# Moving work of the first blocks off VectorE: maxima and masks to TensorE, low parts of weights and numerators to accumulating transfers

## The chip, the cores and the metric

The kernel runs on one core of a Trainium2 chip. The metric is device time in microseconds (us) of one launch, as the median of several runs. The engines have one instruction queue each and run it strictly in order: TensorE (PE in the profile; PEld is its weight load), VectorE (DVE), ScalarE (ACT), GpSimd (POOL) and SyncE (SP). In this kernel SP and POOL only issue transfers (DMAs), apart from a few fills by POOL at the start. Transfers that add into their destination ("accumulating") are issued by POOL.

## The reference, cut to what matters

```python
B, H, S, D = 8, 8, 576, 64
# attention: two parts, added
s  = scale * q_d @ k_d.T                      # q, k, v averaged over groups of 4 rows: 144 x 144
out_d = softmax(s) @ v_d                      # repeated 4 times along the rows
s  = where(|row - col| < 4, scale * q @ k.T, -1e9)
out_local = softmax(s) @ v                    # softmax subtracts the row's maximum, divides by sum + 1e-9
x = (repeat(out_d, 4) + out_local).transpose(0, 2, 1, 3).reshape(4608, 512)
# two-layer network with a rational activation
h = x @ w_in                                  # 512 x 2048
P = a0 + a1*h + a2*h**2 + a3*h**3
Q = 1 + |b0|*|h| + |b1|*h**2
out = (P / (Q + 1e-6)) @ w_out                # 2048 x 512
```

The weights come as 64-bit floats; everything else is 32-bit. All products are carried with close to 32-bit accuracy.

## The kernel before, in words

**Blocks and steps.** The 4608 rows of x are cut into nine blocks of 512: the first 512 rows of each of the eight batches, and a ninth with the 64 rows that each batch leaves over. A block has 16 steps, one for each 128 columns of `w_in`; step n makes `h(n)` (128 x 512, in one of two PSUM banks), `middle(n)` makes the activation from it, and `o(n)` multiplies it with 128 rows of `w_out` and adds into four PSUM banks. `o(n)` stands two steps behind `h(n)` (`LAG`). There are 144 steps.

**Accuracy by two parts.** Fast matmuls take operands rounded to a shorter type (float32r). So each operand is split into a high part (the rounded value) and a low part (what the rounding left), and three products are added: high x high, low x high, high x low, 12 matmuls of 128 x 512 for `h(n)` (L843) and 12 for `o(n)` (L923). Block 0 (steps below `NAT` = 16) makes `h` otherwise: with the unsplit 32-bit `w_in` and x, in 4 slow matmuls (L831, two records each).

**Weights.** `weights(w, f, spot)` fetches 1 MB of 64-bit weights (two steps' worth) into a staging place, and ScalarE (L356) and VectorE (L359, L362) put the exact 32-bit value together from the two halves (`wb`). `parts` splits it: ScalarE copies it into the high tile `wh` (L376), VectorE subtracts, low = exact - high (L379). For `w_out` this is done at once, for `w_in` after block 0 has used the exact value. The exact value lies in the room of the low part.

**Middle.** `middle(n)` has four ScalarE reads of the PSUM bank (|h|, h squared, a3*h+a2, a1*h+a0, all L856), a logarithm and an exponential for the reciprocal of Q, and seven VectorE operations: L871, then the numerator in L876 (multiply by h squared) and L877 (add `u` = a1*h+a0), then L883 (the high part of the activation, `g`), L886, L891, L892 (its low part).

**Attention.** The local scores are made in ten windows of 64 rows per pair of heads, 128 x 640 in two PSUM banks. In batch 0 (the start, before any `h`) `scores` adds the mask on TensorE: four matmuls with an identity (L440) write it into the banks first. `softmax_local` then takes the negative maxima on VectorE (L482), scales them, and ScalarE runs ten small exponentials per pair, 128 x 64 each, with the maximum as bias and the sum taken along (L497). In the other batches `Half.scores` lets VectorE add the mask while it copies the scores out of PSUM (L637), takes maxima (L648), and the ten exponentials read SBUF (L659). `normalize` multiplies by the reciprocal sums: the local part on VectorE, the pooled part on ScalarE (L540), or on VectorE (L548) for the batches in `EP_DVE`, which is batch 0. The mean over 4 rows for the pooled part comes from four loads, three of them accumulating (L419); batch 0 reduces on VectorE (L428). `attend(b)` for batch b+2 is spread over the steps of block b+1, batch 1 over block 0.

**What sets the order.** Every operation is given to a planner with an engine, an assumed cost, what it reads and writes, and here and there a due time. `Plan.run` simulates the engines, taking on each the ready task that is latest against its due time, and this writes one fixed order into each engine's queue. So a change of a cost, a due time (`H0`, `H_FIRST`, `QUAD_GAP`) or a dependence reorders everything; what happens at run time is then decided by the queues and the semaphores alone.

Of the kernel before, what the change touches and what calls it, by code (L numbers as in the profile page):

```python
# [9 lines left out]
F32 = mybir.dt.float32  # L10
BF16 = mybir.dt.bfloat16
# [9 lines left out]
P = 128  # L21
# [162 lines left out]
def attention_moe(  # L184
# [45 lines left out]
    high2, low2, bits2 = [[], []], [[], []], [[], []]  # L230
    for name, parts in (("wh", high2), ("wl", low2)):
        for w in range(2):
            for f in range(0, NFC, 2):
                t = put(f"{name}{w}_{f}", [P, 2, NCC, P], F32R)
                parts[w].append(t)
                if parts is low2:
                    bits2[w].append(put(f"wb{w}_{f}", [P, 2, NCC, P], I32, t.at))
    high, low, bits = (
        [[part(x[w][f // 2], x[w][f // 2].ap[:, f % 2], f % 2 * 4 * DM, 4 * DM) for f in range(NFC)] for w in range(2)]
        for x in (high2, low2, bits2)  # L240
    )

# [10 lines left out]
    maskb = put("maskb", [P, 2, NW // 2 * D], BF16, mt[0].at)  # L253
# [43 lines left out]
    arena = nc.alloc_sbuf_tensor("arena", [P, (top - base) // 4 + 16], I32)  # L297
# [45 lines left out]
    def weights(w, f, spot, due=None):  # L343
        st = spot.ap.rearrange("p n (c f two) -> p n c f two", two=2, c=NCC)
        lo, word = low2[w][f // 2], bits2[w][f // 2]
# [23 lines left out]
        add("DVE", 0.6, upper, (spot,), (lo,))  # L369
        add("DVE", 1.13, lower, (spot, lo), (lo,))  # L370
        if f >= (WO if w else NAT):
            parts(w, f)

    def parts(w, f, due=None):
        hi, lo, word = high2[w][f // 2], low2[w][f // 2], bits2[w][f // 2]
        add("ACT", 0.88, lambda: nc.scalar.copy(out=hi.ap, in_=word.ap.bitcast(F32)), (lo,), (hi,), due=due)  # L376
        add(
            "DVE", 1.13,
            lambda: nc.vector.tensor_tensor(  # L379
                out=lo.ap, in0=word.ap.bitcast(F32), in1=hi.ap.bitcast(F32), op=ALU.subtract  # L380
            ),
            (lo, hi), (lo,), due=due,
        )
# [92 lines left out]
    def softmax_local(c, bk):  # L476
        s = c.slot
        nm, sm = s.nm.ap, s.sm.ap
        view = two(bk)[:, :, : NW // 2 * D].rearrange("p j (c k) -> p j c k", k=D)
# [6 lines left out]
        )  # L486
        add(
# [331 lines left out]
    def h_part(n, f):  # L819
# [5 lines left out]
        if n < NAT:  # L825

            x = xsf[blk.slot][1]
            for c in range(NCC):

                def issue(c=c):  # L830
                    nc.tensor.matmul(  # L831
                        ph.ap, lhsT=bits[0][fc].ap[:, c, :].bitcast(F32), rhs=x.ap[:, c, :],
# [3 lines left out]
                add("PE", 0.858, issue, (low[0][fc], part(x, None, 4 * c * t, 4 * t)), (ph,), due=due_h(n) + 0.05 * c)  # L836
# [21 lines left out]
    def middle(n):  # L858
# [18 lines left out]
        add("DVE", 0.61, lambda: v.tensor_tensor(out=ta.ap, in0=ta.ap, in1=u.ap, op=ALU.add), (ta, u), (ta,))  # L877
        act(0.63, log, tb, tb.ap, AF.Ln, bias=cone)
        act(0.54, tq, log, log.ap, AF.Exp, scale=-1.0)
        if n < WO:  # L880
# [291 lines left out]
```

## Time and profile before

| | |
|---|---|
| median of 3 runs | 971.1 us (970.48 to 972.1) |
| the profiled execution's own time | 970.52 us |
| its span in the trace | 968.5 us |
| TensorE busy | 943.4 us (97%) |
| VectorE busy | 857.2 us (89%) |
| ScalarE busy | 818.0 us (84%) |
| GpSimd busy | 113.8 us (12%) |
| granted TensorE clock, mean | 0.995 |

How to read it: busy times are unions of instruction times; ends of matmuls are modelled, so a TensorE that is paced by waits can still read as busy. "Idle before" is the time in which an engine stood still ahead of an instruction, with the instruction that released it. Lines (L923) are lines of the kernel's file; a group in the profile is one line, engine and shape.

### The profile page before, as it was taken

The page shows a single profiled execution, that of the slowest core. Times are in us where ns is not written, and L with a number is a line of the kernel's source. Part 1 is how long each engine was busy: PE and PEld are TensorE (multiplying, and loading weights), DVE is VectorE, ACT ScalarE, POOL GpSimd, SP SyncE. Part 2 cuts the span into 40 slices and gives each one's busy share as a digit, 9 for nine tenths or more (in the row PEclk, how much of TensorE's full clock was granted, in tenths as well). Part 3 has the DMA queues.
Part 4 walks back from the last instruction along what each step waited for, and adds up shares of the span by engine and source line. Part 5 has one row for each costly group of instructions (what it writes and reads, how often), then busy time and mean ns, then how long its engine had stood idle before and what let it go on. Part 6 is the DMA issues. An engine that isn't in the chain of part 4 may idle for free.

```text
span 968.5 us, 19358 instructions
## 1 busy us (share of the span) xinstructions
PE 943.4 (97%) x7182; PEld 739.6 (76%) x7182; DVE 857.2 (89%) x1450; ACT 818.0 (84%) x2056; POOL 113.8 (12%) x136
## 2 busy tenths in 40 slices
PE   7899999999999999999999999999999999999996
PEld 5555657787877788788877887778878888888885
DVE  6899999999888989898889888898979899988885
ACT  6899898988889897979798978988797977778774
POOL 1212121111202020212111110202021000000000
PEclk9999999999999999999999999999999999999998
DMA  9985453333433344434333433334332010001001
GB/s 296 350 279 118 137 147 85 98 70 83 74 102 57 100 65 110 75 82 75 89 89 72 94 70 106 55 103 72 94 72 57 2 44 1 1 1 44 0 1 44
DMA packets 43166, 85.06 MB, mean 88 GB/s; under 512 B 4864, under 2 KB 25728, under 8 KB 43072
## 3 DMA queue, kind: packets, MB, share of 16 engines
q1 hardware_dynamic: 25344, 63.52, 19.8%
q0 software_dynamic: 17728, 20.31, 15.3%
q8 instruction: 57, 0.93, 0.4%
q14 instruction: 37, 0.30, 0.1%
HBM read 74.37 MB, written 9.44 MB: 87 GB/s over the span
## 4 chain that ended last, share of the span: by engine, by line
PE 40%; DVE 27%; ACT 25%; issue 6%; DMA 1%; DVEq 0%; POOL 0%; ACTq 0%; POOLq 0%; SPq 0%
PE psum L923 18%; PE psum L843 17%; ACT m L856 7%; ACT el L659 7%; DVE g L883 4%; DVE m L886 3%; DVE m L891 3%; ACT epc L523 3%; DVE g L892 3%; DVE m L876 3%; DVE m L871 3%; DVE m L877 3%; ACT gb L856 2%; ACT epc L540 2%; PE psum L831 2%
## 5 line engine op out<-in xcount | busy, mean ns | idle before, releaser
L923 PE MATMUL psum<-wh,g 128*128 128x512 f32 x1152 | 392.9, 404 | 3.2 <-DVE g L892 1.5
L856 ACT ACTIVATE m<-psum,cf 128x512 f32<-128x512 f32 x288 | 212.0, 740 | 63.5 <-PE psum L843 59.4
L923 PEld LDWEIGHTS psum<-wh,g 128*128 128x128 f32 x1152 | 214.1, 188 | 60.6 <-DVE g L892 6.6
L843 PE MATMUL psum<-xs,wh 128*128 128x512 f32 x1024 | 258.8, 393 | 0.1
L923 PE MATMUL psum<-wl,g 128*128 128x512 f32 x576 | 224.3, 390 | 0.0
L843 PEld LDWEIGHTS psum<-xs,wh 128*128 128x128 f32 x1024 | 189.8, 188 | 42.7 <-issue 2.2
L883 DVE TENSOR_TENSOR g<-m,m 128x512 fp32r<-128x512 f32 x144 | 99.5, 691 | 69.0 <-ACT m L856 62.4
L843 PE MATMUL psum<-xs,wl 128*128 128x512 f32 x512 | 137.7, 391 | 0.0
L856 ACT ACTIVATE gb<-psum,cf 128x512 f32<-128x512 f32 x144 | 114.5, 795 | 15.8 <-PE psum L923 15.8
L923 PEld LDWEIGHTS psum<-wl,g 128*128 128x128 f32 x576 | 108.2, 188 | 23.0 <-issue 1.4
L856 ACT ACTIVATE gb<-m,cf 128x512 f32<-128x512 f32 x144 | 106.3, 738 | 19.4 <-DVE m L871 16.8
L419 POOL DMA_DIRECT2D pq<-in_qkp_dram x84 | 74.5, 932 | 389.1 <-DMA pq<-in_qkp_dram 352.0
L856 ACT ACTIVATE m<-gb 128x512 f32<-128x512 f32 x144 | 92.6, 643 | 24.9 <-DVE m L876 23.3
L843 PEld LDWEIGHTS psum<-xs,wl 128*128 128x128 f32 x512 | 95.7, 188 | 20.1
L871 DVE SCALAR_TENSOR_TENSOR m<-m,cf,m 128x512 f32<-128x512 f32 x144 | 107.3, 745 | 1.7 <-ACT m L856 1.6
L877 DVE TENSOR_TENSOR m<-m,gb 128x512 f32<-128x512 f32 x144 | 99.1, 688 | 6.6 <-ACT gb L856 0.4
L886 DVE SCALAR_TENSOR_TENSOR m<-m,g 128x512 f32<-128x512 f32 x144 | 99.4, 690 | 3.5
L892 DVE TENSOR_TENSOR g<-m,m 128x512 fp32r<-128x512 f32 x144 | 98.8, 686 | 2.8
L891 DVE TENSOR_TENSOR m<-m,m 128x512 f32<-128x512 f32 x144 | 99.0, 688 | 2.2
L876 DVE TENSOR_TENSOR m<-m,m 128x512 f32<-128x512 f32 x144 | 98.6, 685 | 0.0
L659 ACT ACTIVATE el<-el,nm 128x64 f32<-128x64 f32 x280 | 93.5, 338 | 3.8 <-DVE nm L653 2.7
L856 ACT ACTIVATE m<-psum 128x512 f32<-128x512 f32 x144 | 86.9, 603 | 0.0
(71 smaller groups left out, 905.9 us busy)
## 6 DMA issues: line engine op xcount, KB each, us to landing
qk<-in_qk_dram SPq DMA_DIRECT2D x32, 590.0 KB, 3.9
pq<-in_qkp_dram POOLq DMA_DIRECT2D x84, 144.0 KB, 3.3
vw<-in_vw_dram SPq DMA_DIRECT2D x32, 320.0 KB, 4.0
out_dram<-xf SPq DMA_DIRECT2D x32, 256.0 KB, 2.4
vpc<-in_vp_dram POOLq DMA_DIRECT2D x42, 168.0 KB, 3.6
sx<-in_w_in_dram SPq DMA_DIRECT2D x5, 1024.0 KB, 13.7
sl<-in_w_out_dram SPq DMA_DIRECT2D x4, 1024.0 KB, 9.5
sx<-in_w_out_dram SPq DMA_DIRECT2D x4, 1024.0 KB, 5.3
```

Of the source, the lines that this page charges most:

```text
L419: lambda d=dst, x=x: nc.gpsimd.dma_start(out=d.ap, in_=x, accum_op=ALU.add),
L659: nc.scalar.activation(out=e[:, n], in_=e[:, n], func=AF.Exp, bias=nm[:, n : n + 1], scale=scale, accum_out=sm[:, n : n + 1],)
L843: nc.tensor.matmul(ph.ap[:, f * t : (f + 1) * t], lhsT=(high, low)[j][0][fc].ap[:, c, :], rhs=blk.x[i].ap[:, c, :] if blk.b is not None el ...
L856: add("ACT", cost, lambda: nc.scalar.activation(out=out_.ap, in_=in_, func=func, **kw), (room_in, cf, *more), (out_,))
L871: lambda: v.scalar_tensor_tensor(out=tb.ap, in0=tq.ap, scalar=b1, in1=tb.ap, op0=ALU.mult, op1=ALU.add),
L876: add("DVE", 0.61, lambda: v.tensor_tensor(out=ta.ap, in0=ta.ap, in1=tq.ap, op=ALU.mult), (ta, tq), (ta,))
L877: add("DVE", 0.61, lambda: v.tensor_tensor(out=ta.ap, in0=ta.ap, in1=u.ap, op=ALU.add), (ta, u), (ta,))
L883: add("DVE", 0.61, lambda: v.tensor_tensor(out=gh.ap, in0=ta.ap, in1=tq.ap, op=ALU.mult), (ta, tq), (gh,))
L886: lambda: v.scalar_tensor_tensor(out=tb.ap, in0=tb.ap, scalar=CONE, in1=gh.ap.bitcast(F32), op0=ALU.add, op1=ALU.mult),
L891: add("DVE", 0.61, lambda: v.tensor_tensor(out=tb.ap, in0=ta.ap, in1=tb.ap, op=ALU.subtract), (ta, tb), (tb,))
L892: add("DVE", 0.61, lambda: v.tensor_tensor(out=gl.ap, in0=tb.ap, in1=tq.ap, op=ALU.mult), (tb, tq), (gl,))
L923: nc.tensor.matmul(ob[sub].ap, lhsT=g[i].ap[:, f0 : f0 + P], rhs=flat((high, low)[j][1][fc].ap), start=(fc == 0 and m == 0), stop=(fc == N ...
```

## The change

Five things are moved, and the planner's numbers are new:

1. Batch 0's softmax (`MINUS`, pairs 0 to 3): two 32-bit matmuls per pair add the negative maxima to the scores in PSUM (`minus`, L542 in the new file). ScalarE then runs two exponentials of 128 x 320 per pair (L549) instead of ten of 128 x 64; VectorE loses the scaling of the maxima and gains a sum over 128 x 640 (L557).
2. Batches 1 and 2 (`PEMASK`) take `scores` and `softmax_local` as batch 0 did: mask by four TensorE matmuls (L491), maxima and ten exponentials from PSUM, no masked copy by VectorE. The two banks stay taken until the exponentials have read them.
3. Low parts of `w_in` (8 pairs of steps): the exact value now lies in the high part's room. ScalarE writes -high into the low room (L424), a transfer adds the exact value (L411), and ScalarE rounds the high room in place later. VectorE's subtraction is gone. For `w_out`, f = 4 to 12 (5 pairs), the exact value lies in the next pair's low room, ScalarE makes high, VectorE writes -high (L390, one input instead of two), and a transfer adds.
4. Numerators of steps 6 to 23 (`UN`): the addition of `u` is a transfer (L954) instead of a VectorE operation.
5. Batch 1's pooled part is normalized on VectorE (`EP_DVE`).

```diff
 def weights(w, f, spot, due=None):
+    whole = f < (0 if w else NAT)
+    added = not whole and ADDED[w] <= f < NFC - 2
+    room = low2[w][f // 2 + 1] if added else (high2 if whole else low2)[w][f // 2]
+    word = aside[w][f // 2 + 1] if added else bits2[w][f // 2]
...
+    if added:
+        add("ACT", 0.88, lambda: nc.scalar.copy(out=hi.ap, in_=word.ap.bitcast(F32)), (room,), (hi,))
+        add("DVE", 0.6, lambda: nc.vector.tensor_single_scalar(out=lo.ap, in_=hi.ap.bitcast(F32), scalar=-1.0, op=ALU.mult), (hi,), (lo,))
+        accumulate(lo, word, room)
...
+def accumulate(lo, word, room, due=None):
+    add("POOL", 1.0, lambda: nc.gpsimd.dma_start(out=flat2(lo), in_=flat2(word).bitcast(F32), accum_op=ALU.add),
+        (room, lo), (lo,), due=due, lag=ALAG)
 def parts(w, f, due=None):                     # DEFER == 1
-    add("ACT", 0.88, lambda: nc.scalar.copy(out=hi.ap, in_=word.ap.bitcast(F32)), (lo,), (hi,), due=due)
-    add("DVE", 1.13, ... lo = word - hi ...)
+    add("ACT", 0.88, lambda: nc.scalar.mul(out=lo.ap, in_=exact, mul=-1.0), (hi,), (lo,), due=due)
+    accumulate(lo, word, hi, due)
+    add("ACT", 0.88, lambda: nc.scalar.copy(out=hi.ap, in_=exact), (hi,), (hi,), due=due)
...
 def softmax_local(c, bk):                      # after the maxima, for pairs in MINUS
+    def minus(j):
+        nc.tensor.matmul(view[:, j], lhsT=ident.ap, rhs=nm[:, 5 * j : 5 * j + 5].unsqueeze(2).broadcast_to([P, NW // 2, D]),
+                         start=False, stop=True, skip_group_check=True)
+    def whole(j):
+        nc.scalar.activation(out=s.el.ap[:, :, c.pos(j), :], in_=view[:, j], func=AF.Exp, scale=scale)
+    for j in range(2): add("PE", 0.56, lambda j=j: minus(j), (s.nm, ident), (bk[j],))
+    for j in range(2): add("ACT", 0.4, lambda j=j: whole(j), (bk[j],), (s.el,))
+    add("DVE", 0.74, ... sm = sum of el ...)
...
 def middle(n):
-    add("DVE", 0.61, lambda: v.tensor_tensor(out=ta.ap, in0=ta.ap, in1=u.ap, op=ALU.add), (ta, u), (ta,))
+    if UN[0] <= n < UN[1]:
+        add("POOL", 0.95, lambda: nc.gpsimd.dma_start(out=ta.ap, in_=u.ap, accum_op=ALU.add), (ta, u), (ta,), lag=ULAG)
+    else: ... as before
...
 def attend(b):
-                half_.scores(c, bk)
+                if b in PEMASK:
+                    scores(c, bk)
+                    softmax_local(c, bk)
+                else:
+                    half_.scores(c, bk)
...
-H0 = 25.89
-H_FIRST = 6.93
+H0 = 16.61
+H_FIRST = 7.57
-QUAD_GAP = 43.57
+QUAD_GAP = 43.21
-EP_DVE = (0,)
+EP_DVE = (0, 1)
+ULAG = 5.0
+UN = (6, 24)
+ALAG = 6.5
+DEFER = 1
+MINUS = (0, 1, 2, 3)
+ADDED = (99, 4)
+PEMASK = (1, 2)
```

How the order moves, at three places. In these rows a name ends in its buffer's number, `out<-in`; numbers differ between the two kernels. First ScalarE's queue from the first exponentials on (`el` is the local, `epc` the pooled exponentials of the pairs of batch 0, `eptc` and `et` their transposes). Before:

```order
L497 ACTIVATE el_151,sm_140<-psum,nm_136 128x64 x5
L497 ACTIVATE el_156,sm_141<-psum,nm_137 128x64 x5
L497 ACTIVATE el_151,sm_140<-psum,nm_136 128x64 x5
L497 ACTIVATE el_156,sm_141<-psum,nm_137 128x64 x5
L497 ACTIVATE el_162,sm_142<-psum,nm_138 128x64 x5
L523 ACTIVATE epc_146,sm_140<-psum,nm_136 128x3x48 x3
L523 ACTIVATE epc_146,sm_141<-psum,nm_137 128x3x48 x3
L497 ACTIVATE el_162,sm_142<-psum,nm_138 128x64 x5
```

and now:

```order
L549 ACTIVATE el_167<-psum 128x5x64 x2
L549 ACTIVATE el_172<-psum 128x5x64 x2
L599 ACTIVATE epc_162,sm_156<-psum,nm_152 128x3x48 x3
L599 ACTIVATE epc_162,sm_157<-psum,nm_153 128x3x48 x3
L549 ACTIVATE el_178<-psum 128x5x64
L549 ACTIVATE el_183<-psum 128x5x64
L549 ACTIVATE el_178<-psum 128x5x64
L549 ACTIVATE el_183<-psum 128x5x64
L363 ACTIVATE sx_189<-sx_189 128x1024
```

Forty small exponentials have become eight, and the first weights' conversion (L363) now follows them directly.

Second VectorE's queue between the two halves of batch 0: the normalization of the second half (`sm`, `epc`, `el`), the first weights (`wb`), the outputs of the first half (`xf`). Before, from the last normalization on:

```order
L548 TENSOR_TENSOR epc_169<-epc_169,sm_143 128x9x48
L558 TENSOR_TENSOR el_167<-el_167,sm_143 128x640
L359 TENSOR_SCALAR wb_0_73<-sx_173 128x1024
L359 TENSOR_SCALAR wb_0_89<-sl_175 128x1024
L362 SCALAR_TENSOR_TENSOR wb_0_73<-sx_173,wb_0_73 128x1024
L590 TENSOR_TENSOR xf_1_107<-psum,up_144 128x48
```

and now:

```order
L624 TENSOR_TENSOR epc_185<-epc_185,sm_159 128x9x48
L634 TENSOR_TENSOR el_183<-el_183,sm_159 128x640
L340 MEMSET cf 128x1
L366 TENSOR_SCALAR wb_0_65<-sl_191 128x1024
L366 TENSOR_SCALAR wb_2_83<-sx_190 128x1024
L666 TENSOR_TENSOR xf_1_123<-psum,up_160 128x48
```

The first weight pair (`wb_0_81` in the new file) is converted ahead of this normalization and no longer between it and the outputs.

Third GpSimd's queue where the numerators begin. Rows with `pq` and `vpc` are the accumulating loads of batch 1's second half. Before:

```order
L419 DMA vpc<-in_vp_dram 112x384
L419 DMA pq_149<-in_qkp_dram 128x288
L419 DMA pq_154<-in_qkp_dram 128x288
L419 DMA pq_149<-in_qkp_dram 128x288
L419 DMA pq_154<-in_qkp_dram 128x288
```

and now, with the low part of `w_out` (`wl_6_70`) and the numerators of steps 6, 7 and 8 (`m_132`, `m_133`, `m_132`):

```order
L411 DMA wl_6_70<-wa_4_116 128x1024
L954 DMA m_132<-gb_142 128x512
L470 DMA pq_165<-in_qkp_dram 128x288
L470 DMA pq_170<-in_qkp_dram 128x288
L470 DMA pq_165<-in_qkp_dram 128x288
L470 DMA pq_170<-in_qkp_dram 128x288
L954 DMA m_133<-gb_143 128x512
L470 DMA pq_165<-in_qkp_dram 128x288
L954 DMA m_132<-gb_142 128x512
```

Between two steps' numerators stand loads that wait for the ones ahead of them.

More of the change, by code (lines that the diff above doesn't have):

```diff
@@ L252, in attention_moe @@
     identb = put("identb", [P, P], BF16)
[L253 removed]
+    maskb = put("maskb", [P, 2, NW // 2 * D], BF16)
     maskd = put("maskd", [P, NW // 2, D], BF16)
@@ L368, in weights @@
         add("ACT", 0.94, scaled, (spot,), (spot,))
[L369 to L372, printed above, removed]
+        add("DVE", 0.6, upper, (spot,), (room,))
+        add("DVE", 1.13, lower, (spot, room), (room,))
+        if added:
+            hi, lo = high2[w][f // 2], low2[w][f // 2]
+            if f >= CAST:
+                add(
+                    "POOL", 1.0, lambda: nc.gpsimd.dma_start(out=flat2(hi), in_=flat2(word).bitcast(F32)),
+                    (room,), (hi,), lag=CLAG,
+                )
+            else:
+                add("ACT", 0.88, lambda: nc.scalar.copy(out=hi.ap, in_=word.ap.bitcast(F32)), (room,), (hi,))
+            if NEG:
+                add(
+                    "DVE", 0.6,
+                    lambda: nc.vector.tensor_single_scalar(
+                        out=lo.ap, in_=hi.ap.bitcast(F32), scalar=-1.0, op=ALU.mult
+                    ), (hi,), (lo,),
+                )
+            else:
+                add("ACT", 0.88, lambda: nc.scalar.mul(out=lo.ap, in_=hi.ap.bitcast(F32), mul=-1.0), (hi,), (lo,))
+            accumulate(lo, word, room)
+        elif not whole:
+            hi, lo = high2[w][f // 2], low2[w][f // 2]
+            add("ACT", 0.88, lambda: nc.scalar.copy(out=hi.ap, in_=word.ap.bitcast(F32)), (lo,), (hi,))
+            add(
+                "DVE", 1.13,
+                lambda: nc.vector.tensor_tensor(
+                    out=lo.ap, in0=word.ap.bitcast(F32), in1=hi.ap.bitcast(F32), op=ALU.subtract
+                ),
+                (lo, hi), (lo,),
+            )
@@ L486, in softmax_local @@
         )
+        if first:
+            def minus(j):
+                nc.tensor.matmul(
+                    view[:, j], lhsT=ident.ap,
+                    rhs=nm[:, 5 * j : 5 * j + 5].unsqueeze(2).broadcast_to([P, NW // 2, D]),
+                    start=False, stop=True, skip_group_check=True,
+                )
+            def whole(j):
+                nc.scalar.activation(out=s.el.ap[:, :, c.pos(j), :], in_=view[:, j], func=AF.Exp, scale=scale)
+            for j in range(2):
+                add("PE", 0.56, lambda j=j: minus(j), (s.nm, ident), (bk[j],))
+            for j in range(2):
+                add("ACT", 0.4, lambda j=j: whole(j), (bk[j],), (s.el,))
+            add(
+                "DVE", 0.74,
+                lambda: nc.vector.tensor_reduce(
+                    out=sm[:, :NW], in_=s.el.ap.rearrange("p c j k -> p (c j) k"), axis=AX, op=ALU.add
+                ),
+                (s.el,), (s.sm,),
+            )
+            return
         add(
```

70 lines of the change are left out of this document (38 added, 32 removed).

## The prediction

> **What bounds the kernel now.** I read the busy time by stretch first, then TensorE's waits, then its timeline at the start, and from there the queue of the engine it waited for. Busy time in five stretches (columns: length; busy time and count of PE, PEld, DVE, ACT, POOL; granted clock; DMA share; GB/s):
>
> ```profile
> 40.00:50.00 10.00, 7.53 (x110) 4.16 (x103) 7.56 (x12) 6.25 (x11) 3.97 (x4) 0.83 1.08 352
> 60.00:100.00 40.00, 38.41 (x236) 24.57 (x233) 39.87 (x68) 39.87 (x109) 5.28 (x6) 1.00 0.51 147
> 100.00:140.00 40.00, 38.78 (x289) 23.59 (x287) 38.72 (x67) 36.08 (x99) 8.09 (x9) 1.00 0.54 139
> 140.00:180.00 40.00, 39.22 (x320) 28.30 (x321) 38.64 (x62) 35.72 (x74) 2.48 (x3) 1.00 0.42 112
> 254.60:358.54 103.94, 103.52 (x840) 83.34 (x839) 91.25 (x161) 90.58 (x243) 15.47 (x18) 1.00 0.38 83
> ```
>
> The last row is one block in the steady state: 103.94 us, TensorE busy for 103.52 of it, VectorE for 91.25. There TensorE is the bound, and the change touches nothing after step 23 (about 210 us). In 60 to 180 all three engines are nearly full; the question is who waits for whom. TensorE's waits from 44.2 to 260 us (us in total, times, longest):
>
> ```profile
> PE psum L831 <- DVE xf L590: 2.5, 1, 2.5
> PE psum L831 <- DVE wb L362: 1.5, 2, 1.3
> PE psum L831 <- ACT gb L856: 1.0, 1, 1.0
> PE psum L923 <- DVE sm L535: 0.9, 1, 0.9
> PE psum L679 <- ACT eptc L716: 0.7, 1, 0.7
> PE psum L923 <- DVE g L883: 0.3, 1, 0.3
> ```
>
> So from 44.30 on TensorE stands still for only 4.4 us (1.5 + 1.0 + 0.9 + 0.7 + 0.3), besides 1.7 us lost to the clock (0.83 in 40 to 50). Everything else that can be won lies ahead of 44.30 us. TensorE's timeline (start, duration, line, operands, count, idle before):
>
> ```profile
> 6.53 0.48 PE L440 MATMUL psum<-maskb,identb 64*64 64x320 bf16 x4
> 6.80 0.98 PE L450 MATMUL psum<-qk 64*64 64x64 f32 x40
> 34.94 2.81 PE L831 MATMUL psum<-xf,wb 128*128 128x512 f32 x6 [1.00 <-DVE xf L590]
> 44.30 10.52 PE L831 MATMUL psum<-xf,wb 128*128 128x512 f32 x20 [2.47 <-DVE xf L590]
> ```
>
> The first products of `h` start at 34.94 with the pairs that are ready, and the run that never breaks again starts at 44.30, released by VectorE's `xf` of batch 0's second half. The end of the span is 44.30 plus TensorE's remaining work plus those few waits: **what moves 44.30 moves the end one for one, and TensorE work added later is paid in full.** VectorE's queue up to there:
>
> ```profile
> 7.89 0.82 DVE L482 TENSOR_REDUCE nm<-psum 128x10 f32<-128x640 f32 x1 [1.75 <-PE psum L450]
> 8.63 1.34 DVE L428 TENSOR_REDUCE pq<-qk 128x288 f32<-128x1152 f32 x1
> 9.89 0.81 DVE L482 TENSOR_REDUCE nm<-psum 128x10 f32<-128x640 f32 x1
> ...
> 17.39 0.60 DVE L512 TENSOR_REDUCE nm<-psum 128x3 f32<-128x432 f32 x1
> 17.91 0.16 DVE L489 TENSOR_TENSOR nm<-nm,scales 128x10 f32<-128x10 f32 x1
> ...
> 19.50 0.17 DVE L534 TENSOR_SCALAR sm<-sm 128x13 f32<-128x13 f32 x1 [1.30 <-ACT epc L523]
> ...
> 22.93 0.60 DVE L512 TENSOR_REDUCE nm<-psum 128x3 f32<-128x432 f32 x1
> ...
> 31.32 0.69 DVE L359 TENSOR_SCALAR wb<-sx 128x1024 int32<-128x1024 int32 x1
> ...
> 32.53 1.22 DVE L362 SCALAR_TENSOR_TENSOR wb<-sx,wb 128x1024 int32<-128x1024 int32 x1
> 33.67 1.67 DVE L590 TENSOR_TENSOR xf<-psum,up 128x48 f32<-128x48 f32 x6
> ...
> 43.83 1.67 DVE L590 TENSOR_TENSOR xf<-psum,up 128x48 f32<-128x48 f32 x6
> ```
>
> From starts that follow each other without a gap come the prices used below: a maximum over 128 x 640 takes 0.74 (7.89 to 8.63), a mean over four rows 1.26 (8.63 to 9.89), a pooled maximum 0.52, the eight operations that normalize a half 3.43 (19.50 to 22.93), a shift of weights 0.60 (two from 31.32 to 32.53), the or of the two words 1.14, the six outputs of a half 1.6. Between 10 and 28 us VectorE has gaps: ScalarE's exponentials are what it waits for.
>
> **Part 1, the start.** Groups of instructions (busy, mean ns | idle before):
>
> ```profile
> L497 ACT ACTIVATE el<-psum,nm 128x64 f32<-128x64 f32 x40 | 12.1, 415 | 8.9 <-DVE nm L489 8.9
> L856 ACT ACTIVATE m<-psum 128x512 f32<-128x512 f32 x144 | 86.9, 603 | 0.0
> L376 ACT CAST wh<-wb 128x1024 fp32r<-128x1024 f32 x16 | 16.7, 1063 | 1.3 <-DVE wb L362 1.2
> L540 ACT ACTIVATE epc<-epc,sm 128x144 f32<-128x144 f32 x84 | 27.9, 440 | 0.0
> L523 ACT ACTIVATE epc<-psum,nm 128x144 f32<-128x144 f32 x96 | 35.1, 401 | 0.0
> L548 DVE TENSOR_TENSOR epc<-epc,sm 128x432 f32<-128x432 f32 x4 | 2.4, 609 | 0.3
> ```
>
> Forty small exponentials hold ScalarE for 12.1 us. Eight of 128 x 320 replace them; between the 0.30 of 128 x 64 (12.1/40) and the 0.60 of 128 x 512 I take 0.48 each, 3.8 together. The ends for what this gives the start are therefore 0 and 8.3 us. VectorE gains four sums over 128 x 640 (as maxima, 0.74) and loses four small scalings, so I walk its new queue from 7.89, where nothing has changed yet. Until the first normalization: 4 maxima 2.96, 3 means 3.78, 2 sums 1.48, 2 pooled maxima 1.04, 2 scalings 0.24, which is 9.5 us and ends at 17.4 (19.5 before). ScalarE is in time: its six pooled exponentials follow the scalings at 15.4 and need 2.2 (35.1/96 each). Normalization to 20.8; 2 sums, 2 pooled maxima, 2 scalings 2.8; the first weight pair, now here, 0.60 + 1.14; the second normalization 3.43: that is 28.8, against 31.32. So 2.5 us are certain as far as the durations hold, and VectorE, not ScalarE, is what they end on. Then only two shifts (1.2) stand ahead of the first half's outputs instead of two shifts and an or: 30.0, or 30.2 with the copies of `up` on ScalarE, which the first -high copy now precedes; before 33.67. After the outputs come four ors, two shifts and a subtraction, 6.9 us, to 38.7. There ScalarE is later: two -high copies of 1.0 (row L376) and a conversion stand ahead of the second half's `up`, and I put the outputs at 39.7, against 43.83. **Gain 4.1**, TensorE's run from 40.2. The new 32-bit matmuls of `minus` are at nothing here: their cover is TensorE's own emptiness, since until 34.94 it mostly runs fillers between the scores. Ends 2.5 (the later part lost again) and 8.3.
>
> **Part 2, masks on TensorE.** Four mask matmuls start at 6.53 and the scores behind them at 6.80: 0.27 a pair. Eight pairs of batches 1 and 2: **+2.2**, in full, since TensorE has no slack there. Ends: 0 (all in waits) and 8 x 0.48 = 3.8, the rows' whole duration.
>
> **Part 3, VectorE in block 0 and 1.**
>
> ```profile
> L877 DVE TENSOR_TENSOR m<-m,gb 128x512 f32<-128x512 f32 x144 | 99.1, 688 | 6.6 <-ACT gb L856 0.4
> L379 DVE TENSOR_TENSOR wl<-wb,wh 128x1024 fp32r<-128x1024 f32 x16 | 19.5, 1220 | 0.4 <-ACT wh L376 0.4
> L637 DVE TENSOR_TENSOR el<-psum,maskd 128x640 f32<-128x640 f32 x28 | 22.9, 817 | 0.0
> ```
>
> In block 0 it loses ten numerators (steps 6 to 15) of 0.69, eight subtractions of 1.22, four masked copies of 0.82, and in five pairs of `w_out` 1.22 becomes 0.69 (one input; price of the shift row), and gains four pooled normalizations of 0.61 (L548): 6.9 + 9.8 + 3.3 + 2.7 - 2.4 = 20.3 us less, where 60 to 180 shows 2.8 us of idle time in 120. An engine off the bound gives nothing by itself; what it gives is TensorE's waits for it, 1.5 + 0.9 + 0.3: **gain 2.7**, all there is. Ends 0 and 2.7.
>
> **Part 4, ScalarE in block 0.** Eight -high copies of 1.06 are added (the later copy was there before), 8.5; batch 1's pooled normalization leaves, 84 instructions in 27.9 for 28 pairs, so 1.0 a pair, 4.0. Its exponentials now read PSUM and not SBUF:
>
> ```profile
> L659 ACT ACTIVATE el<-el,nm 128x64 f32<-128x64 f32 x280 | 93.5, 338 | 3.8 <-DVE nm L653 2.7
> ```
>
> 12.1/40 against 93.5/280, times 40, saves 1.3. Sum 8.5 - 4.0 - 1.3 = +3.2. Idle in 60 to 180: 0.13 + 3.92 + 4.28 = 8.3. It fits, if the planner's order leaves the gaps usable, so I take **0**; the ends are 0 and +3.2, since ScalarE is the one that is full from 60 to 100.
>
> **Part 5, transfers in the middle.** GpSimd's queue (two rounds of accumulating loads, each waiting for the one before) and its DMA queue (packets, MB, share of 16 engines):
>
> ```profile
> 79.98 1.79 POOL L419 DMA_DIRECT2D pq<-in_qkp_dram  x2 [24.91 <-DMA pq<-in_qkp_dram]
> 83.69 0.86 POOL L419 DMA_DIRECT2D pq<-in_qkp_dram  x1 [1.93 <-DMA pq<-in_qkp_dram]
> ...
> 87.33 0.89 POOL L419 DMA_DIRECT2D pq<-in_qkp_dram  x1 [1.49 <-DMA pq<-in_qkp_dram]
> q0 software_dynamic: 17728, 20.31, 15.3%
> ```
>
> The second load into a tile is issued 3.7 us after the first (79.98 to 83.69, 83.69 to 87.33): 144 KB from issue to the next user. The queue's 20.31 MB took 15.3% of 16 x 968.5 us, 117 engine-us per MB, so 256 KB take 1.9 us on 16 engines against 1.1: a numerator 4.5 us, a low part of 512 KB 6.5. The twelve products of one `h` late in the trace, in the chain of waits:
>
> ```profile
> 782.41 2.72 PE psum L843 x12
> ```
>
> From the last product of `h(n)` to `o(n)` it now takes four ScalarE reads 2.4 (0.60 each), a multiplication 0.7, the transfer 4.5, the multiplication by the reciprocal 0.7, together 8.3. Two steps of 6.5 (103.94/16) less 2.7 leave 10.3, so the transfer is hidden with 2.0 to spare; its cover is the products of the two following steps, and if that goes `o(n)` is late and with it the release of the banks of `g`. Low parts have longer: those of `w_in` until block 1, those of `w_out` two steps. **0**; ends 0 and 18 steps x half of the 3.8 that the transfer is longer than the addition (two steps are in flight), 34. Near the lower end, by that spare. All 31 new transfers, 11.5 MB, are 84 us of all 16 engines at that price, over some 170 us whose DMA share is about 0.5: close to full, but only if they all stay as slow as the small packets of the rows.
>
> VectorE was busy for 39.87 of 40 us while these issues took 0.86 to 0.89 each, so an issue beside a full VectorE costs what it costs anywhere. Against that stands a rule of the Trainium skill: SBUF — State Buffer, "Who interferes with whom", says that GpSimd, which writes the descriptors of the transfers it issues, is locked out while VectorE runs a one-input instruction in a two-port mode. By the rows the sum has nothing for it; by the rule each numerator could come one such instruction later, an estimate of 18 x 0.35 = 6.3 us on top if none of it is hidden.
>
> **The sum.** 970.52 - 4.1 + 2.2 - 2.7 = 965.9 for the execution profiled, which lies 0.6 below the median of the runs; so 966.5.
>
> **Rivals.**
> - *The start gains less, and ScalarE takes the rest.* The second half's outputs wait for ScalarE's copies and conversions, and block 0 becomes ScalarE's: -2.5 + 2.2 - 0.7 + 2.0, about 972. For it: ScalarE idles 0.13 us in 60 to 100. Against: its gaps of 3.92 and 4.28 later. Chance 0.14, no change.
> - *The start gains more.* The clock's 1.7 us go too, because TensorE no longer stands still for 2.5 us just ahead of 44.3, and the start's gain lies half way to its upper end: -6.2 - 2.7 - 1.7 + 2.2, 962.7 by the median. Chance 0.14, faster.
> - *Numerators come late (slower).* GpSimd's queue runs in order: step 7's numerator stands behind four loads of `pq`, and the first of them waits for a transfer that SP starts only when TensorE has read the old `pq`. GpSimd already waited 24.91 us there. On VectorE the multiplication by the reciprocal waits, and everything queued behind it, the other step's low part and the attention's maxima. Each us beyond the spare of 2.0 costs TensorE half a us per step. It decides from 0.36 us a step: 18 x 0.36 = 6.5 eats the gain of 4.6 and 1.9 more; at 1 us a step the time is 984.5. Against: the loads' 3.7 us and the numerators' 4.5 leave room. Chance 0.13.
> - *Masks hold the banks.* Two PSUM banks stay taken through ten exponentials (3.0 us) instead of one copy (0.8) per pair; if TensorE's next scores wait for them in all eight pairs, that is 8 x 2.2 = 18 us; products of `h` and `o` stand between, so I put half of it: 975. Chance 0.03.
> - *GpSimd's issues are held up by VectorE.* VectorE's shifts and sign changes, 0.6 to 0.7 each, stand between the steps' operations; an issue that waits for one of them makes its numerator that much later, and exposed by half in 18 steps that is 6.3 us: 972.8, within the bound of no change. Against it the rows' even 0.86 to 0.89. Chance 0.02. (The rule weighed in part 5.)
>
> **How the numbers follow.** The forecast has 0.54, between 964 and 969. A measurement of this kernel can hardly tell 0.2% (1.9 us) from no change. Faster: 0.54 + 0.14 = 0.68; no change 0.14 + 0.02 = 0.16; slower 0.13 + 0.03 = 0.16. The range holds the first three cases and the mild part of the others: 960 to 974.5.
>
> **What would show it.** The profile after should have TensorE's long run of L907 start near 40 us; VectorE without gaps from 8 to 28 us; VectorE's idle time in 60 to 180 up from 2.8 to over 15 us; TensorE's waits for VectorE gone; GpSimd's numerators from issue to VectorE's L959 under 6 us; a block from 254 us on unchanged at 103.9. The forecast is wrong if TensorE's waits name `m` by a DMA, if the run starts after 42, or if ScalarE has no idle time up to 180 us.

## The result, and the profile after

The changed kernel takes 985.35 us (median of 4 runs, 984.33 to 986.08) against 971.6 for the kernel before on the same chip; the ratio is 1.0147, with a 95% interval of 1.0135 to 1.0159. It is 1.5% slower. The forecast was 966.5, in a range up to 974.5. Ratios here and below are over undisturbed runs alone, so a median divided by a median can differ from them a little. The profiled execution has a span of 982.6 us against 968.5, so 14.1 us are to be found.

Busy time by stretch, columns as in the prediction. The last row is a stretch in the steady state, as long as a block of the kernel before:

```profile
60.00:100.00 40.00, 38.75 (x189) 23.63 (x188) 36.53 (x63) 38.67 (x98) 7.88 (x9) 0.97 0.78 221
100.00:140.00 40.00, 36.10 (x311) 21.62 (x309) 31.03 (x50) 33.36 (x87) 13.09 (x14) 0.96 0.97 223
140.00:180.00 40.00, 37.11 (x283) 25.94 (x283) 31.26 (x57) 35.75 (x80) 14.55 (x16) 1.00 0.83 177
180.00:220.00 40.00, 36.66 (x221) 29.47 (x225) 27.05 (x47) 32.52 (x91) 11.43 (x13) 0.91 0.57 114
254.60:358.54 103.94, 103.94 (x844) 84.11 (x843) 90.76 (x160) 90.67 (x245) 16.34 (x19) 1.00 0.39 85
```

In the steady stretch TensorE gets through as many matmuls as before (844 against 840). From the stores of block 1 (286.35 us) to those of block 6 (806.99 us) a block takes 104.1 us, where it took 103.9. So 12.9 of the 14.1 us are lost ahead of 286 us, and 1.2 us in the blocks behind. VectorE did become lighter: 836.2 us busy in all, where it had 857.2. In 60 to 180 it is busy for 98.8 of 120 us, where it had 117.2. But there TensorE and ScalarE are busy for less of the time as well: all three wait. The DMA share went from about 0.5 to 0.78, 0.97 and 0.83. TensorE's waits from 44.2 to 260 us:

```profile
PE psum L985 <- DVE g L959: 6.8, 3, 4.7
PE psum L907 <- ACT gb L932: 3.0, 1, 3.0
PE psum L985 <- DMA wl<-wa: 2.4, 1, 2.4
PE psum L491 <- ACT el L573: 1.1, 1, 1.1
PE psum L518 <- ACT el L573: 0.7, 1, 0.7
```

That is 14.0 us where 4.4 stood. Where they lie, in the timeline, with the start's long run ahead of them:

```profile
41.68 8.82 PE L907 MATMUL psum<-xf,wb 128*128 128x512 f32 x20 [1.67 <-DVE xf L666]
58.86 1.79 PE L907 MATMUL psum<-xf,wb 128*128 128x512 f32 x2 [3.01 <-ACT gb L932]
...
129.43 0.50 PE L985 MATMUL psum<-wl,g 128*128 128x512 f32 x1 [2.41 <-DMA wl<-wa]
...
183.34 0.76 PE L985 MATMUL psum<-wh,g 128*128 128x512 f32 x1 [4.67 <-DVE g L959]
183.90 0.63 PE L985 MATMUL psum<-wl,g 128*128 128x512 f32 x1
184.33 0.63 PE L985 MATMUL psum<-wh,g 128*128 128x512 f32 x1
```

Around each of the three longest waits the granted clock falls to half for some 3.4 or 6.8 us, and matmuls start 0.43 us apart instead of 0.23. Three stretches, with the clock in the third column from the end:

```profile
58.86:62.50 3.64, 3.64 (x7) 2.27 (x8) 3.19 (x6) 2.61 (x3) 0.00 (x0) 0.54 1.07 300
129.43:134.20 4.77, 4.77 (x12) 3.14 (x13) 1.26 (x3) 0.53 (x2) 0.86 (x1) 0.65 1.07 297
181.00:189.00 8.00, 5.66 (x14) 4.48 (x15) 5.67 (x9) 4.76 (x11) 2.34 (x3) 0.57 0.56 136
```

The clock takes 1.7 + 1.7 + 3.4 us there (length times what is missing to 1), 0.7 of it while TensorE stood still anyway, against 1.7 before. The sum: start -2.6 (41.68 against 44.30), waits +9.6, clock +4.4, masks +2.2 (the prediction's price, not measured), together +13.6, near the 12.9 us that lie ahead of 286 us.

What was late? GpSimd's queue ahead of the longest wait, and the VectorE row that waited:

```profile
163.42 0.86 POOL L470 DMA_DIRECT2D vpc<-in_vp_dram  x1 [0.61 <-DMA vpc<-in_vp_dram]
164.02 2.09 POOL L411 DMA_DIRECT2D wl<-wb  x2
166.84 0.86 POOL L411 DMA_DIRECT2D wl<-wb  x1 [0.73 <-DMA vpc<-in_vp_dram]
167.68 0.90 POOL L470 DMA_DIRECT2D vpc<-in_vp_dram  x1
173.56 0.90 POOL L954 DMA_DIRECT2D m<-gb  x1 [4.99 <-ACT m L932]
182.50 0.69 DVE L959 TENSOR_TENSOR g<-m,m 128x512 fp32r<-128x512 f32 x1 [4.46 <-DMA m<-gb]
```

The numerator issued at 173.56 is used at 182.50. Three low parts of 512 KB were issued ahead of it; `w_in`'s low parts come in bursts, 31 to 42 us, 120 to 126, 164 to 168. The row of ScalarE at 133.73 shows the second kind of lateness, a 1 MB load of weights on SP's queue, issued at 121.97; in the kernel before, a load of the same weights in this stretch landed after 5.0 us:

```profile
133.73 1.14 ACT L363 ACTIVATE sx<-sx 128x1024 f32<-128x1024 f32 x1 [4.24 <-DMA sx<-in_w_in_dram]
```

From issue to landing, least, median and longest of all transfers of a line: numerators (L954), low parts (L411), loads of weights after (L356) and before (L349), in this order:

```profile
DMA to landing us min/median/max: 3.2/3.5/11.4
DMA to landing us min/median/max: 4.9/11.2/14.7
DMA to landing us min/median/max: 5.6/13.6/25.7
DMA to landing us min/median/max: 5.0/10.0/20.2
```

Queues in the stretch from 118 to 142 us (packets, MB, share of 16 engines), before and then after:

```profile
q1 hardware_dynamic: 961, 2.95, 31.9%
q0 software_dynamic: 864, 0.89, 28.2%
```

```profile
q0 software_dynamic: 1124, 2.97, 66.7%
q1 hardware_dynamic: 887, 3.25, 37.8%
```

Together that is 104.5% of the 16 engines by the profile's count, where 60% stood: the engines are full there. From this come two theories: **Q**, the numerators stand behind low parts in GpSimd's one DMA queue; **B**, the bursts of low parts take the engines from everybody, and the loads of weights come late. A third, **S**: masks, subtraction or the new order cost it.

### The profile page after: what moved, and what is told of

Same layout as the page of the kernel before. It is cut to its first block, busy times and chain, and to the rows that moved or that the text cites. A ratio compares the mean times of both kernels' runs of the same rounds, so it can differ in the third digit from the quotient of the medians.

```text
span 982.6 us, 19282 instructions
## 1 busy us (share of the span) xinstructions
PE 948.5 (97%) x7168; PEld 742.1 (76%) x7168; DVE 836.2 (85%) x1420; ACT 812.2 (83%) x1980; POOL 142.1 (14%) x167
## 3 DMA queue, kind: packets, MB, share of 16 engines
q0 software_dynamic: 22192, 31.84, 21.2%
## 4 chain that ended last, share of the span: by engine, by line
PE 45%; DVE 23%; ACT 20%; DMA 6%; issue 5%; DVEq 0%; POOL 0%; ACTq 0%; POOLq 0%; SPq 0%
PE psum L985 20%; PE psum L919 19%; ACT m L932 6%; ACT el L735 5%; DVE g L959 3%; DVE m L962 3%; DMA sl<-in_w_out_dram 3%; DVE m L967 3%; DMA m<-gb 3%; ACT epc L599 3%; DVE g L968 3%; DVE m L952 2%; ACT gb L932 2%; DVE m L947 2%; DVE m L956 2%
## 5 line engine op out<-in xcount | busy, mean ns | idle before, releaser
L959 DVE TENSOR_TENSOR g<-m,m 128x512 fp32r<-128x512 f32 x144 | 99.5, 691 | 80.4 <-ACT m L932 65.7
L968 DVE TENSOR_TENSOR g<-m,m 128x512 fp32r<-128x512 f32 x144 | 98.6, 685 | 3.6
L956 DVE TENSOR_TENSOR m<-m,gb 128x512 f32<-128x512 f32 x126 | 86.7, 688 | 7.5 <-ACT gb L932 0.9
L735 ACT ACTIVATE el<-el,nm 128x64 f32<-128x64 f32 x200 | 66.7, 335 | 2.7 <-DVE nm L729 1.9
```

What stands on the lines that cost most here:

```text
L735: nc.scalar.activation(out=e[:, n], in_=e[:, n], func=AF.Exp, bias=nm[:, n : n + 1], scale=scale, accum_out=sm[:, n : n + 1],)
L959: add("DVE", 0.61, lambda: v.tensor_tensor(out=gh.ap, in0=ta.ap, in1=tq.ap, op=ALU.mult), (ta, tq), (gh,))
L968: add("DVE", 0.61, lambda: v.tensor_tensor(out=gl.ap, in0=tb.ap, in1=tq.ap, op=ALU.mult), (tb, tq), (gl,))
```

## The experiments

Ratios are to the kernel before on the same chip, with their 95% intervals.

**1. Numerators back on VectorE**, in place, the order of all queues kept.

```diff
-lambda: nc.gpsimd.dma_start(out=ta.ap, in_=u.ap, accum_op=ALU.add)
+lambda: v.tensor_tensor(out=ta.ap, in0=ta.ap, in1=u.ap, op=ALU.add)
```

> The 18 numerators of steps 6 to 23 are added by VectorE again, at the place in the order where the transfer was issued; the 13 low parts stay transfers and the order of everything else stays. Theory Q (the numerators stand behind low parts of 512 KB in GpSimd's one queue, TensorE waits for them at three steps and runs at half clock after each long wait): the 6.8 us of waits for L959 and the 3 to 5 us of half clock behind them go, the 2.4 us wait for w_out's low part stays: 973 to 976. Theory L (a numerator by transfer takes longer than its spare time whatever stands in the queue): the same, 973 to 976, so this run tells neither from the other. Theory S (the loss is the masks, the subtraction or the new order, and the waits for L959 only show where it comes out): 982 to 986.

980.87 us, 1.0098 [1.0084, 1.0111]. A miss for all the theories: only 4.5 us come back. The waits for numerators are gone, and the late load of weights stops everything instead, ScalarE first, TensorE behind it:

```profile
135.99 1.10 ACT L363 ACTIVATE sx<-sx 128x1024 f32<-128x1024 f32 x1 [5.95 <-DMA sx<-in_w_in_dram]
138.62 0.46 PE L518 MATMUL psum<-pq 64*64 64x144 f32 x4 [4.22 <-ACT el L573]
```

So Q alone is not the cause.

**2. `w_in`'s 8 low parts on VectorE**, in place: `tensor_tensor(out=lo.ap, in0=word, in1=lo, op=ALU.add)` for the transfer in `accumulate`. **3. All 31 additions on VectorE**, in place.

> The 8 low parts of w_in that fall in steps 6 to 23 are added by VectorE, at the same place in the order; the numerators and the 5 low parts of w_out stay transfers. Q: with no 512 KB transfers in a burst ahead of them the numerators land in 3.5 to 6 us and TensorE no longer waits for L959 at 140, 162 and 183 us; 971 to 975. L: the numerators are late by themselves; the waits for L959 stay near 6.8 us in all, 981 to 985. S: 982 to 986.

> All 31 additions by VectorE at the places of the transfers; what stays of the change is the subtraction by TensorE, the masks of batches 1 and 2, and the new order. Q and L: no wait for a transfer is left, VectorE is as loaded as before; start gain of 2.6 and masks of 2.2 us about cancel: 969 to 973. S: still 980 or more. If the new order needs the lighter VectorE, its waits come back at other steps and the time lies between, 974 to 978.

974.71 us, 1.0035 [1.0018, 1.0053], and 981.43, 1.0098 [1.0084, 1.0112]. In both, the additions at the old places hold back VectorE's `xf`, and the long run starts late:

```profile
45.63 10.52 PE L909 MATMUL psum<-xf,wb 128*128 128x512 f32 x20 [3.35 <-DVE xf L668]
```

```profile
45.27 8.82 PE L907 MATMUL psum<-xf,wb 128*128 128x512 f32 x20 [3.34 <-DVE xf L666]
```

In 3 TensorE waits 11.8 us for VectorE besides (`g`, L968 and L959): this order was written for a light VectorE. So although the time of 3 is what S expected, 3 tells nothing on S by itself. 2 wins 10.6 us, as Q has it; B would have it too. Its trace is of an execution of 977.25 us, one of the longer ones (971.4 to 978.25); that one starts 4 us late.

**4. The subtraction of batch 0's maxima alone**, on the kernel before: the `minus` branch of `softmax_local` and `MINUS = (0, 1, 2, 3)`; `maskb` gets a place of its own in memory, and the planner orders everything anew.

> The kernel before with the subtraction of batch 0's maxima by TensorE alone (masks, low parts, numerators and the planner's numbers as before). If the start's gain of 2.6 us that the changed kernel showed (TensorE's long run from 41.7 instead of 44.3 us) comes from the subtraction: run from 41 to 42 us and 968 to 969.5. If the prediction's 4.1 us was right for the subtraction and the new order took part of it back: run from 40 to 40.5 and 967 to 968. If the gain came from what was moved and not from the subtraction: 970.5 to 972.

976.45 us, 1.0039 [1.0026, 1.0053]; a miss. The run starts at 42.34, two us earlier than before, and the time is longer. VectorE is busy for 40.00 of the 40 us from 60 on, and at 195.03 TensorE waits 3.96 us for `g`. So an earlier start need not last to the end. Whether the full VectorE takes it back or the new order does was not separated; run 13 shows that an order alone can cost as much.

**5. As 2, but the first low part stays a transfer. 6. As 2, but the first three stay.**

> As the run with w_in's low parts on VectorE, but the first of the 8, issued at 31.3 us, stays a transfer: in that run VectorE's addition at this place held back xf and the long run of TensorE began at 45.6 us instead of 41.7. Expected of Q (numerators behind low parts in one queue) and of a second theory B (the low parts fill the 16 DMA engines, so that 1 MB loads of weights on SP's queue land late and ScalarE, VectorE and TensorE wait for those) alike: run from 41.7 again and 974.7 - 3.9 = 970 to 972. If the late start cost nothing in the end, because VectorE bounds the stretch to 220 us anyway: 974 to 976.

> The changed kernel, but of w_in's 8 low parts only the three issued at 31 to 42 us stay transfers; the five of the bursts at 120 to 125 and 164 to 167 us are added by VectorE at the same places. If the bursts cause the loss (the late load of w_in at 133.7, the late numerators at 140 and 183 with the half clock behind them): run from 41.7, the wait of 3.0 us at 58.9 stays, 971 to 974. If the loss is the three at the start, which crowd the loads of 40 to 60 us: 978 to 982.

975.33 us, 1.0045 [1.0028, 1.0062], and 977.22, 1.0067 [1.0049, 1.0084]. In 5 the run still starts at 44.26, since the second and third addition stand ahead of `xf` too, so it does not test what it was made for. In 6 it starts at 42.33, and TensorE's wait for ScalarE at 59.4 (2.93 us) is back; ScalarE for its part waits up to 3.5 us for a load of `w_out` there. 6 is a miss for both its theories. Moving the five low parts of the later bursts wins 8 us, so these cost most. Moving the other three too wins some 2 us more (run 2), but there the intervals overlap, so that the first burst costs time by itself is not shown.

**7. Eight more transfers on the kernel before**, behind each subtraction that makes a low part of `w_in`: `nc.gpsimd.dma_start(out=hi, in_=lo, accum_op=ALU.add)`.

> The kernel before with 8 accumulating transfers of 512 KB more in GpSimd's queue, each issued right behind the subtraction that makes a low part of w_in (it adds the low part into the high part, so the weights used in blocks 1 to 7 are not the reference's; VectorE's work stays). No numerators stand in that queue. Q: nothing of the first blocks waits behind them but loads that have time, 970.5 to 972.5. B: loads of weights come late, ScalarE waits 3 to 6 us for one, and TensorE behind it, with half clock after it: 974 to 980.

976.28 us, 1.0051 [1.0034, 1.0067]. It is as B has it by the time. Its trace is of the fastest of the four executions (973.4), and there the clearest wait is TensorE's own for one of the new transfers (3.0 us for `wh<-wl`); ScalarE's waits for weights are 2.0 in all. Eight such transfers cost about 5 us here without any numerators; it does not tell by which way.

**8. `w_in`'s low parts at an eighth of their bytes**, in the changed kernel; order and issues stay.

```diff
-nc.gpsimd.dma_start(out=flat2(lo), in_=flat2(word).bitcast(F32), accum_op=ALU.add)
+nc.gpsimd.dma_start(out=flat2(lo)[:, :128], in_=flat2(word)[:, :128].bitcast(F32), accum_op=ALU.add)
```

> The changed kernel, but the 8 transfers for w_in's low parts carry 128 of 1024 elements a partition, so 64 KB instead of 512 KB (seven eighths of these low parts lack the added words). Order, issues, and every other engine's work as in the changed kernel. Q and B both put the loss on the bytes: 968 to 972. If the issues or the order cost the time: 982 to 986.

969.43 us, 0.9984 [0.9974, 0.9993]. This is the test that S fails: masks, subtraction, order, issues and 18 numerators are all still there, and the loss is gone. The bytes of eight transfers cost 16 us. In 118 to 142 us the engines are still at 96% here (61.0 and 35.4), so a full stretch by itself does not make the loss. What goes is the lateness: ScalarE's waits for loads of weights fall from 11.0 to 3.6 us, VectorE's for numerators from 8.5 to 1.9. What stays is a wait of 2.0 us of TensorE for `wl<-wa`, a low part of `w_out`: these are whole here, and their cover of two steps is too short in a stretch so full.

**9. The same bytes by another queue:** each of these low parts moved by two plain copies issued by ScalarE.

> The changed kernel, but each of w_in's 8 low parts is moved by two plain copies of 512 KB issued by ScalarE on its own queue (nothing is added, so these low parts are not the reference's). The bytes on the 16 DMA engines stay about the same, GpSimd's queue holds the numerators, w_out's 5 low parts and the pooled loads alone. Q: numerators land in 3.5 to 6 us, 970 to 975, ScalarE's 16 issues of about 0.35 us each hidden in its idle time. B: the loads of weights are as late as before, 978 to 984.

1021.78 us, 1.0522 [1.0506, 1.0538]. A miss for both, and inconclusive by a fault of the design: the second copy writes where the first does, so its issue waits for the first to land, and ScalarE, which issues, stands still with everything queued behind it:

```profile
32.73 8.17 ACTq L414 DMA_DIRECT2D wl<-wb  x2
40.95 0.28 ACT L843 ACTIVATE up<-psum 64x144 f32<-64x144 f32 x1 [8.08 <-DMA wl<-wb]
```

**10. Numerators at an eighth of their bytes**, low parts whole. **11. Numerators on VectorE, low parts at an eighth.** They complete a table with 1 and 8.

> The changed kernel, but the 18 transfers of numerators carry 64 of 512 elements a partition (seven eighths of the odd terms are left out of the numerators of steps 6 to 23); all low parts are full transfers. If numerators are late because they stand behind low parts in one queue, small ones are as late as full ones: 983 to 986, TensorE waits 5 to 7 us for L959. If it is the numerators' own bytes: 978 to 982, as with numerators on VectorE.

> Numerators on VectorE, and w_in's 8 low parts as transfers of 64 KB (seven eighths of these lack the added words): no numerator is a transfer and no w_in low part is large. If the low parts' bytes cost time by late loads of weights, the 11 us between this and the run with numerators on VectorE and full low parts is their price without any queue: 968 to 972. If most of that run's 980.9 came from VectorE's added load: 976 to 981.

| us | `w_in`'s low parts whole | an eighth |
|---|---|---|
| numerators by transfer | 985.35 | 969.43 |
| numerators by transfer, an eighth | 982.14, 1.0122 [1.0105, 1.0139] | |
| numerators on VectorE | 980.87 | 970.15, 0.9990 [0.9979, 1.0001] |

With no numerator in any queue the low parts still cost 10.7 us; with the numerators, 16. The numerators cost 4.5 us beside whole low parts and nothing beside small ones. The waits for loads of weights, first in run 1 and then in run 11, show where the 10.7 us come from:

```profile
  ACT sl L363: 7.4, 4
  ACT sx L363: 6.0, 1
```

```profile
  ACT sx L363: 1.2, 1
  ACT sl L363: 0.6, 2
```

TensorE's waits for ScalarE are 9.8 us in run 1 and 1.1 in run 11, and the half clock around them takes 6.8 us in run 1 and nothing in run 11. That is B. The median of the loads, 13.7 us in run 1, is 10.8 in run 11 (10.0 in the kernel before). For Q, the small numerators' time to land in run 10 was:

```profile
DMA to landing us min/median/max: 2.1/2.3/10.7
```

So 10.7 us by their longest, nearly the 11.4 of whole ones; it was issued at 125.88, behind three low parts (118.25, 119.75, 122.87), and TensorE still waits 4.3 us for L959. That is what Q says. But 10 itself missed: with the place in the queue kept, 3.2 of the 4.5 us came back. So the place explains a part of the 4.5 us, the numerators' own bytes another, and the split is not settled, since the two intervals nearly touch. Either way it is the smaller part of the loss.

**12. The low parts of `w_in` spread in time.** A field `nb` tells the planner that a task may not start before a time; all transfers and bytes stay.

```diff
+nb = due - 30.0        # in parts(): for the copy, the transfer and the high part
-at = 0.0
+at = t.nb              # in Plan.run, release()
```

> The changed kernel, but the planner may start the making of each of w_in's 8 low parts no sooner than 30 us (of its own time) ahead of its use, so the transfers come one by one some 12.6 us apart instead of in bursts of 2 and 3; all bytes as in the changed kernel. If bursts of 512 KB transfers are the cause: 969 to 974. If the bytes cost time wherever they lie: 980 to 986.

973.66 us, 1.0034 [1.0017, 1.0052]: 11.7 of the 13.8 us are back with all the bytes. The eight low parts are now issued at 113.8, 142.4, 146.4, 162.5, 167.1, 202.7, 208.4 and 215.6 us, none at the start and none less than 4 us behind another. The DMA share in 60 to 180 is 0.86, as in the changed kernel, but the longest numerator takes 8.1 us instead of 11.4, and the median low part 7.6 instead of 11.2. So it is when the bytes are moved, and not how many: spread and held back they are nearly hidden. The rule moves the whole order with them, and how much of the 11.7 us is owed to that is not separated. TensorE's waits from 44.2 us on:

```profile
PE psum L986 <- DVE g L960: 2.8, 4, 1.2
PE psum L986 <- DMA wl<-wa: 2.3, 1, 2.3
PE psum L908 <- DVE wb L369: 2.1, 1, 2.1
PE psum L986 <- DVE g L969: 0.2, 1, 0.2
```

**13. The same rule on the kernel before**, without any transfer.

> The kernel before with the same rule for w_in's low parts (VectorE subtracts them as before, no transfers): what is gained by their later place alone. No transfer is added, and VectorE has the same work before step 24: 969 to 973; faster than 969 only if the early low parts held up the first steps.

975.53 us, 1.0053 [1.0036, 1.0069]; a miss. Its run starts at 45.34; a new order can cost this kernel some 5 us by itself.

**14. Numerators alone:** all 13 low parts by VectorE, the planner told so (`DEFER = 0`, `ADDED = (99, 99)`). **15. As 12, with `w_out`'s low parts on VectorE. 16. As 14, with 12's rule. 17. As 16, with 20 us instead of 30.**

> The changed kernel with all 13 low parts subtracted by VectorE, by the planner's own order for it; the numerators of steps 6 to 23 are the only transfers of the change. If numerators without low parts in their queue land in time: 968 to 972, no wait of TensorE for L959 over 1 us. If they are late by themselves: 976 to 985.

> Late, spread low parts of w_in by transfer as in the run before, and w_out's 5 low parts subtracted by VectorE, all by the planner's order for it. The wait of 2.3 us for a low part of w_out at 122.8 and the half clock behind it go: 967 to 971, faster than both kernels. If VectorE's 5 added subtractions come late at 90 to 140 us: 971 to 976.

> Numerators by transfer alone, all low parts by VectorE, those of w_in no sooner than 30 us ahead of their use. Against the run with early low parts on VectorE (973.3) it tells whether their place costs anything without transfers: 967 to 971 if the late places free VectorE in the first steps, 972 to 975 if not.

> The fastest version so far with the low parts of w_in no sooner than 20 instead of 30 us ahead of their use. If its gain is the mechanism (no bursts of large transfers, VectorE free of low parts in the first steps): 967 to 971. If it was one lucky order: 971 to 977.

973.33 us, 1.0025 [1.0013, 1.0037]; 979.13, 1.0084 [1.0068, 1.0100]; 968.70, 0.9979 [0.9969, 0.9988]; 968.37, 0.9968 [0.9956, 0.9981]. 14 is somewhat over its expectation. Its trace, in which TensorE waits for L959 only 2.4 us in all and 1.1 at the longest, is of its fastest execution (969.73), so what the other executions wait for is not known. In 15, a miss, low parts and numerators meet again in the new order: VectorE waits 5.2 us for one numerator, TensorE 5.6 behind it. In 16 and 17 only numerators are left in the queue, and both are faster than the kernel before.

**18. As 16, with the numerators on VectorE too** (`UN = (24, 24)`): no transfer of the change is left, only subtraction, masks, new numbers and the rule of 12.

> As the fastest version so far (all low parts by VectorE, those of w_in late), with the numerators of steps 6 to 23 on VectorE too: of the change only the subtraction and the masks on TensorE stay. If transferred numerators are worth their 11 us of VectorE's time: 971 to 976. If VectorE had the time anyway: 967 to 970.

967.53 us, 0.9961 [0.9948, 0.9975]: the fastest version, 0.4% faster than the kernel before. The numerators' transfers were worth nothing. VectorE carries the additions as before, 117.1 us in 60 to 180, and TensorE waits 2.6 us for it behind the start, where it was 2.7 before:

```profile
40.86 8.82 PE L909 MATMUL psum<-xf,wb 128*128 128x512 f32 x20 [1.20 <-DVE xf L668]
```

```profile
PE psum L763 <- ACT et L794: 2.7, 1, 2.7
PE psum L909 <- DVE wb L369: 1.0, 2, 0.6
PE psum L987 <- DVE g L961: 0.7, 1, 0.7
PE psum L647 <- DVE xf L668: 0.5, 1, 0.5
PE psum L987 <- DVE g L970: 0.4, 1, 0.4
```

Its parts, the subtraction alone (4) and the late low parts alone (13), were each slower. What it has is the start: its long run begins 3.4 us earlier than before, and its span is 2.9 us shorter. The masks alone, and masks with subtraction without the rule, were not tried, so which of them lets the early start last is open; a lucky order is not excluded either.

## Why the prediction was wrong

- **Part 5, the transfers: the step that failed.** It set them at 0. Its prices for one transfer by itself were fair: a numerator 4.5 us (3.5 by the median), and 84 us of all 16 engines for the 11.5 MB (60 by the share of GpSimd's queue, which went from 15.3 to 21.2% of the span). What failed was to spread these over "some 170 us whose DMA share is about 0.5". They come in bursts: in 118 to 142 us the engines were full, low parts took 11.0 and 12.9 us there by their medians (`wa` and `wb`) where 6.5 was set, and one numerator 11.4. The sentence "low parts have longer" asked only who waits for the low parts; it did not ask who stands behind them. Two did: the loads of weights on the other queue (10.7 us, runs 1 and 11) and the numerators (4.5 us, partly by their place in the same queue). And "two steps" were too short for one low part of `w_out` (2.4 us, 2.0 in run 8). The changed kernel's queue on GpSimd shows `w_in`'s low parts two and three close together.
- **The slower rival** named the right victim, the numerators, and 984.5 us is by chance close. Its cause, the loads of `pq`, was wrong (run 8 has them all, and no loss). That the bytes delay other queues was no rival at all.
- **The rival of the held banks** priced the wait of the next scores for the exponentials at up to 18 us. The trace has this wait once, 1.1 us (L491 for `el` L573), and about the same in run 8 (1.0).
- **Clock.** That the clock can halve behind a wait was seen in the trace before (2.47 us ahead of 44.30, 0.83 in 40 to 50) and priced only as a gain. It made 4.4 us of the loss. TensorE: Matmul & The Clock Gate, in the Trainium skill, Part 1, has the clock fall after an idle window of some 3.4 us and return after one that is busy. The stretches at half clock agree in length (3.4 us and twice that). But a wait of 2.41 us ahead of 129.43 was enough to be followed by one, so a wait shorter than the window is no safe one; nor does each wait bring one, since in run 3 the clock stays at 1.00 behind a wait of 3.34 us.
- **Part 1: right in kind, too large.** The run starts at 41.68, a gain of 2.6 and not 4.1. The missing 1.5 us arise at the first half's outputs, which were put at 30.2 and came at 31.94. They waited for ScalarE's copies of `up`, behind a conversion of weights that had itself waited 0.81 us for a load:

```profile
31.94 1.68 DVE L666 TENSOR_TENSOR xf<-psum,up 128x48 f32<-128x48 f32 x6 [1.14 <-ACT up L839]
```

Six kernels with the same order up to there (this one and runs 1, 6, 8, 10 and 11) show 40.7 to 43.4 in one profile each, so 1.5 us are also within what single profiles scatter. With the low parts out of the start (run 12) it is 40.18, as forecast. But run 4 shows the larger error: a gain at the start moves the end one for one only if the steps behind it let it. In run 4 it was lost again, in run 18 it was kept.
- **Part 2** (+2.2) was not measured alone; run 8, with all the masks, is no slower than the kernel before.
- **Part 3: the lightening was right, its worth wrong.** VectorE is busy for 21.0 us less in all (20.3 forecast for block 0), and idle in 60 to 180 for 21.2 us (over 15 forecast). But 6.8 us of waits for `g` came in the place of the 2.7 that were to go, most of it for numerators that had not landed. Run 18 has VectorE as full as before, TensorE waits for it as long as before (2.6 us), and it is the fastest: the lightening was not what a gain hung on.
- **Part 4: right, as far as the trace shows.** ScalarE has 12.2 us idle in 60 to 180, and TensorE's waits for it at 58.86 (3.0 us) and 138.38 (0.7) stand behind its own waits for loads of weights.
- **The rule on ports weighed in part 5:** the numerators' issues took 0.867 us by their median, as the loads' 0.86 before; nothing of it is seen, and no run here takes away the VectorE instructions that the rule names.

## What to carry to other kernels

A transfer that is off the critical path still holds its place in a queue and its share of the 16 engines. Price a set of new transfers by the burst in which the order issues them, against what the engines have to carry in that stretch, and ask for each who stands behind it, on its own queue and on the others. Transfers with a late deadline are worth holding back until near that deadline: a scheduler that starts them as soon as it can makes the bursts. For work of an engine the same rule is to be tried, not assumed: it won in run 16 against 14, and cost 0.5% in run 13.

## What the runs showed of the hardware

- Transfers on SP's hardware queue and on GpSimd's software queue share the same engines: in the stretch where GpSimd's took 66.7% of their time, a load of 1 MB on SP's took 11.7 us, where it took 5.0 before, and the median of all those loads rose from 10.0 to 13.6. The Trainium skill says so (DMA: Bandwidth & Descriptors, "Issuing engines are not separate DMA queues"), and the runs agree.
- A small transfer issued behind large ones in the software queue can take as long as they do: in run 10 32 KB landed after 2.3 us by the median, and after 10.7 behind three of 512 KB.
- In this kernel an engine that issues a transfer onto a destination that another is still writing waits for that one to land, with everything queued behind: 8.08 us on ScalarE (run 9).
